# Seven input transfers per head pair in place of twelve, in a fused attention and two-MLP kernel

## Chip, cores and metric

The kernel runs on one core of a Trainium2 chip. The metric is the device time of one execution in microseconds (us). The kernel before was run three times: 1204.57, 1206.59 and 1207.52 us, a median of 1206.59.

## What is computed

Three stages follow each other: attention with a threshold, then two layers of a gated MLP form. All inputs and outputs are fp32.

```
scores = q k^T / sqrt(64)                      (batch 4, heads 8, seq 576, dim 64)
scores below max - tau are dropped; attn = softmax(scores); a = attn v
x   = a as (2304 tokens, 512)
x1  = (s * relu(x @ w_in)^2 + b) @ w_out         (512 -> 2048 -> 512)
h   = x1 @ w2_in;  out = (h * tanh(softplus(h))) @ w2_out
```

## The kernel before, in words

Attention works on **pairs** of heads: 4 batches of 4 pairs, 16 pairs in all. A pair's queries are handled in 9 ticks of 128 columns (`scores`, lines 236 to 279): ticks 0 to 3 are head 0, ticks 5 to 8 are head 1, and tick 4 holds the last 64 queries of both. A tick's exponentials are transposed seven ticks later (`weights_t`, line 283) and multiplied with v one tick after that (`product`, line 303). After the last product of a pair, `split_x` (line 314) writes its result as a high and a low part.

For precision, fp32 products are made of fp32r parts: an operand is split into `hi` (rounded) and `lo` (the rest). For each pair `prep_qk` (line 196) does this for k and for q. TensorE transposes the raw tile in five pieces of 128 columns (line 204), which ends in the PSUM tile `tpk` or `tpq`. `load_raw` for the following pair is issued (line 205). ScalarE copies 576 columns to `hi` (line 208) and VectorE subtracts to get `lo` (line 209). Then `move` brings halves of 64 partitions to the tiles `Q`, `KH` and `KL` of one of two sets (`self.sets`, lines 139 to 148). For the first pair (`pr` 0) the moves are copies on ScalarE, VectorE and GpSimd (lines 228 to 232); for all others they are DMAs on the SP queue (line 226): six for k, and six for q, since head 1 of q is cut in two pieces per half.

`load_raw` (line 160) brings a pair's raw tiles: k in 5 transfers (lines 176 and 184 to 187), q in 3 (lines 176, 178, 179), v in 4 (lines 171 to 173), all on the SP queue. In `attention` (line 324) the k and q of pair 0 are loaded first (line 332), then three scalars, then v. In the loop the next pair's k is prepared after tick 2, its q after tick 4, and its v is loaded after tick 8 (lines 349 to 354). The v tiles are two buffers, so the v of pair p goes into the tile that pair p-2 used.

The first stage of the program runs attention for pairs 0 to 3 alone, beside a generator that reads weights (`split_w`, line 46): one DMA into `wraw` (line 57), one pass on ScalarE (line 62), three on VectorE (lines 64 to 66), a copy on ScalarE (line 69) and a subtraction on GpSimd (line 70). These pieces are used in the first MLP (`moe1`, line 151, its products in line 403), which from pair 4 on is woven with attention in a fixed proportion (lines 612 to 626). For batches 1 to 3 the split weights come back from DRAM (`w<-w`, line 395). When attention is done, the weights of the second MLP are split, and `moe2` (line 469) runs at the end.

Every engine, and the SP queue, takes its instructions in order. The order in each of them is not the program's alone: the build places instructions by a timeline of its own, with the program's order as priority (line 687).

```
687    with _tile.TileContext(nc, schedule_with_timeline_sim=True) as tc:
```

Of the kernel before, what the change touches and what calls it, by code (L numbers as in the profile page):

```python
# [8 lines left out]
F32 = mybir.dt.float32  # L9
# [10 lines left out]
class Fused:  # L20
# [12 lines left out]
    def consts(self, pool):  # L33
        nc = self.nc
        i2 = pool.tile([P, 192], F32, name="ident")
        self.ident, self.swap = i2[:, 0:128], i2[:, 64:192]
        make_identity(nc, self.ident)
        nc.gpsimd.tensor_copy(i2[:, 128:192], i2[:, 0:64])
        self.tau_c = pool.tile([P, 1], F32, name="tau_c")
        self.s_c = pool.tile([P, 1], F32, name="s_c")  # L40
        self.b_c = pool.tile([P, 1], F32, name="b_c")
        self.colsum = pool.tile([P, 4], F32, name="colsum")
        self.cb = pool.tile([P, 4], F32, name="cb")
# [88 lines left out]
    def attn_alloc(self):  # L132
        nc = self.nc
        self.sets = []

# [13 lines left out]
        self.qk = {}  # L149
        for n in "qk":  # L150
            t = self.qk[n] = self.at.tile([P, 5, 2, 64], F32, name=f"raw{n}", bufs=1)
            nc.gpsimd.memset(t[64:128, 4], 0.0)
# [7 lines left out]
    def load_raw(self, pr, nm):  # L160
# [4 lines left out]
        src = {"q": self.q, "k": self.k, "v": self.v}[nm]  # L165
        h2 = src[b, 2 * p:2 * p + 2]
        rem = h2[:, 512:576, :].rearrange("h r d -> r h d")
        if nm == "v":
            t = self.vs[pr % 2]
            for h in range(2):  # L170
                nc.sync.dma_start(t[:, h, 0:4, :], h2[h, 64 * h:64 * h + 512, :].rearrange("(p c) d -> p c d", c=4))
            nc.sync.dma_start(t[0:64, 0, 4, :], h2[0, 512:576, :])
            nc.sync.dma_start(t[64:128, 1, 4, :], h2[1, 0:64, :])
        else:
            t = self.qk[nm]
            nc.sync.dma_start(t[:, 0:4, 0, :], h2[0, 0:512, :].rearrange("(p c) d -> p c d", c=4))
            if nm == "q":
                nc.sync.dma_start(t[:, 0:4, 1, :], h2[1, 0:512, :].rearrange("(p c) d -> p c d", c=4))
                nc.sync.dma_start(t[0:64, 4, :, :], rem)
            else:  # L180


                full = h2[1, 64:576, :].rearrange("(p c) d -> p c d", c=4)
                nc.sync.dma_start(t[64:128, 0:4, 1, :], full[0:64])
                nc.sync.dma_start(t[0:64, 1:5, 1, :], full[64:128])
                nc.sync.dma_start(t[0:64, 0, 1, :], h2[1, 0:64, :])
                nc.sync.dma_start(t[0:64, 4, 0, :], h2[0, 512:576, :])
# [7 lines left out]

    def prep_qk(self, pr, n):


        nc = self.nc
        raw = self.raws.pop((pr, n))  # L200
        Q, KH, KL, _ = self.sets[pr % 2]
        tp = self.s_tile(f"tp{n}{pr}")
        for c in range(5):
            nc.tensor.transpose(tp[:, c * 128:c * 128 + 128], raw[:, c].rearrange("p h d -> p (h d)"), self.ident)
        self.load_raw(pr + 1, n)
        hi = self.at.tile([P, 576], F32R, tag="hi", name=f"hi{n}{pr}", bufs=1)
        lo = self.at.tile([P, 576], F32R, tag="lo", name=f"lo{n}{pr}", bufs=1)
        nc.scalar.copy(hi, tp[:, :576])
        nc.vector.tensor_tensor(lo, tp[:, :576], hi.bitcast(F32), op=ALU.subtract)
        for h, (own, oth) in enumerate((HALVES, HALVES[::-1])):  # L210
            for half, t in ((own, hi), (oth, hi if n == "k" else lo)):
                if n == "k":
                    parts = [(KH[h], 0, 576, 0)]
                else:
                    parts = [(Q, 0, 576, 0)] if h == 0 else [(Q, 0, 512, 704), (Q, 512, 576, 128)]
                for dst, a, z, o in parts:
                    self.move(pr, dst[half, a + o:z + o], t[own, a:z], t is hi)
            if n == "k":
                self.move(pr, KL[h][own, :], lo[own, :], None)

    def move(self, pr, dst, src, early):


        nc = self.nc
        if pr:
            nc.sync.dma_start(dst.bitcast(F32), src.bitcast(F32))
        elif early is None:
            nc.gpsimd.tensor_copy(dst, src.bitcast(F32))
        elif early and dst.shape[-1] > 64:
            nc.scalar.copy(dst, src.bitcast(F32))  # L230
        else:
            nc.vector.tensor_copy(dst, src.bitcast(F32))
# [91 lines left out]
    def attention(self):  # L324
# [11 lines left out]
        self.load_raw(0, "v")  # L336
        for n in "kq":
            self.prep_qk(0, n)
        fin = todo = None
        tes = {}  # L340
        for k in range(N + LAG + 2):
            pr, ti = divmod(k, 9)
            if k < N:
# [5 lines left out]
                if pr + 1 < self.B * self.NP and ti in (2, 4, 8):  # L349
                    if ti == 8:  # L350
                        self.load_raw(pr + 1, "v")
                    else:
                        self.prep_qk(pr + 1, "kq"[ti // 2 - 1])
                        yield 500
# [8 lines left out]
            if todo:  # L363
# [8 lines left out]
                if tc == 8:  # L372
                    self.split_x(tp)
            todo = (prj, ci, tnew) if 0 <= j < N else None
# [317 lines left out]
```

## Time and profile before

| | |
|---|---|
| median of three runs | 1206.59 us |
| the profiled execution, its own time | 1204.01 us |
| its span, first to last instruction | 1201.8 us |
| TensorE busy | 1145.2 us, 95% |
| VectorE / ScalarE / GpSimd busy | 626.1 / 529.7 / 427.3 us |

In the rows, PE is TensorE, PEld its weight loads, DVE is VectorE, ACT is ScalarE, POOL is GpSimd, and SPq the issuing queue of SyncE. L204 is line 204. A busy PE is not a PE at its peak, since matmuls are pipelined and their ends are modelled; the distance between starts tells what one costs in a stream. A releaser is inferred from semaphore events.

### The profile page before, as it was taken

How to read it: one execution, taken by the hardware profiler on the slowest of the kernel's cores; microseconds unless marked ns; L12 is line 12 of the kernel's file. 1: busy time of each engine (PE TensorE's matmuls, PEld its weight loads, DVE VectorE, ACT ScalarE, POOL GpSimd, SP SyncE). 2: the span in 40 equal slices, each digit the busy share in tenths (PEclk: the TensorE clock that was granted, in tenths of full speed). 3: DMA queues.
4: the chain of work that ended last, by engine and by line, in shares of the span. 5: the costliest groups of instructions: out<-in, count | busy, mean ns of one | idle time of the engine just before them, and what ended most of it. 6: DMA issues, size and time to landing. Idle time of an engine off the chain costs nothing.

```text
span 1201.8 us, 19799 instructions
## 1 busy us (share of the span) xinstructions
PE 1145.2 (95%) x7104; PEld 979.2 (81%) x7104; DVE 626.1 (52%) x1505; ACT 529.7 (44%) x1073; POOL 427.3 (36%) x600
## 2 busy tenths in 40 slices
PE   4888999898899999999999999999999999999998
PEld 4666888877678998988988999878888888888886
DVE  5888777878885464655552689964111111111111
ACT  4666666575655544445533465553221221222211
POOL 4566777776644334326422344432000000000000
PEclk8989999999999999999999999999999999999999
DMA  5657466576595455374423898763030020030000
GB/s 128 166 136 183 110 217 184 159 207 173 170 289 156 158 154 159 125 233 140 136 86 106 256 324 283 276 230 105 1 105 1 1 70 1 1 105 1 19 1 35
DMA packets 123667, 161.84 MB, mean 135 GB/s; under 512 B 57393, under 2 KB 78897, under 8 KB 123569
## 3 DMA queue, kind: packets, MB, share of 16 engines
q1 hardware_dynamic: 123568, 160.58, 43.5%
q8 instruction: 56, 0.92, 0.3%
q14 instruction: 43, 0.34, 0.1%
HBM read 107.48 MB, written 30.93 MB: 115 GB/s over the span
## 4 chain that ended last, share of the span: by engine, by line
PE 69%; DMA 10%; DVE 8%; POOL 5%; issue 3%; ACT 2%; SPq 2%; DVEq 0%; ACTq 0%; POOLq 0%
PE o L522 17%; PE h L403 11%; PE y L403 10%; PE hm L493 8%; PE hp L493 8%; PE pv L311 6%; DMA wraw<-in_moe_w_in_dram 4%; PE S L252 4%; DMA wraw<-in_moe_w_out_dram 4%; PE T L289 3%; POOL e L277 3%; DVE wa L64 1%; DMA w<-w 1%; DVE wa L65 1%; DVE wa L66 1%
## 5 line engine op out<-in xcount | busy, mean ns | idle before, releaser
L507 DVE TENSOR_TENSOR g2l<-t,g2h 128x512 fp32r<-128x512 f32 (+1 forms) x80 | 51.9, 648 | 315.4 <-ACT t L506 311.6
L403 PE MATMUL y<-gh,w 128*128 128x288 f32 x768 | 164.6, 300 | 3.1 <-DVE y L450 2.9
L403 PE MATMUL h<-xh,w 128*128 128x288 f32 x768 | 165.5, 301 | 1.9 <-DMA w<-w 1.7
L522 PE MATMUL o<-w2o,g2h 128*128 128x512 f32 x576 | 150.0, 395 | 1.9 <-ACT g2h L505 1.9
L267 DVE SCALAR_TENSOR_TENSOR e<-ns,st,e 128x576 f32<-128x576 f32 x128 | 119.2, 935 | 47.3 <-ACT e L263 33.4
L277 POOL TENSOR_SCALAR e<-e,st 128x576 f32<-128x576 f32 x128 | 127.5, 1005 | 32.3 <-DVE st L272 26.1
L256 DVE TENSOR_SCALAR_CACHE_REDUCE ns<-S 128x576 f32<-128x576 f32 x144 | 107.7, 751 | 54.2 <-PE S L252 53.3
L403 PEld LDWEIGHTS y<-gh,w 128*128 128x128 f32 x768 | 125.8, 188 | 11.1 <-issue 4.4
L403 PEld LDWEIGHTS h<-xh,w 128*128 128x128 f32 x768 | 125.9, 188 | 9.5 <-issue 5.7
L263 ACT ACTIVATE e<-ns,st 128x576 f32<-128x576 f32 x128 | 98.8, 776 | 70.9 <-DVE ns L256 59.6
L522 PEld LDWEIGHTS o<-w2o,g2h 128*128 128x128 f32 x576 | 107.0, 188 | 26.7 <-ACT g2h L505 2.3
L300 ACT COPY te<-T 128x576 f32<-128x576 f32 x144 | 91.1, 632 | 66.6 <-PE T L294 60.5
L258 POOL TENSOR_SCALAR st<-st,tau_c 128x1 f32<-128x1 f32 x144 | 61.1, 426 | 164.9 <-DVE ns L256 140.7
L403 PE MATMUL y<-gl,w 128*128 128x288 f32 x384 | 113.8, 297 | 0.5 <-DVE gl L427 0.5
L252 PE MATMUL S<-KH,Q 128*128 128x288 f32 x320 | 100.3, 329 | 14.6 <-DVE ns L256 5.0
L403 PE MATMUL h<-xl,w 128*128 128x288 f32 x384 | 113.8, 297 | 0.0
L289 PE MATMUL T<-ident,e 128*128 128x128 f32 x576 | 98.3, 279 | 13.8 <-ACT te L300 8.6
L493 PE MATMUL hm<-y,w2i 128*128 128x512 f32 (+1 forms) x480 | 108.4, 372 | 0.0
L493 PE MATMUL hp<-y,w2i 128*128 128x512 f32 (+1 forms) x480 | 107.2, 372 | 0.0
L427 POOL TENSOR_TENSOR gl<-rr,gh 128x288 fp32r<-128x288 f32 x96 | 80.6, 845 | 73.8 <-DVE rr L426 63.2
L311 PE MATMUL pv<-te,rawv 128*64 128x288 f32 x640 | 105.6, 420 | 0.0
L493 PEld LDWEIGHTS hm<-y,w2i 128*128 128x128 f32 x480 | 84.5, 188 | 18.0
(94 smaller groups left out, 2122.7 us busy)
## 6 DMA issues: line engine op xcount, KB each, us to landing
w<-w SPq DMA_DIRECT2D x96, 512.0 KB, 4.2
wraw<-in_moe_w_in_dram SPq DMA_DIRECT2D x64, 256.0 KB, 3.9
w<-wp SPq DMA_DIRECT2D x32, 512.0 KB, 4.0
wraw<-in_moe_w_out_dram SPq DMA_DIRECT2D x64, 256.0 KB, 4.4
KH<-hik SPq DMA_DIRECT2D x60, 144.0 KB, 2.5
y<-yT SPq DMA_DIRECT2D x32, 256.0 KB, 4.0
KL<-lok SPq DMA_DIRECT2D x30, 144.0 KB, 2.7
rawq<-in_q_dram SPq DMA_DIRECT2D x32, 128.0 KB, 3.0
```

What stands on the lines that cost most here:

```text
L252: nc.tensor.matmul(so, Q[:, c0:c0 + 128], kt[:, ks], start=(i == 0), stop=(i == len(terms) - 1))
L256: nc.vector.tensor_scalar(ns.rearrange("p (h n) -> p h n", h=2), sv, -0.125, 3.0e38, op0=ALU.mult, op1=ALU.min, accum_out=nm[:, c1])
L263: nc.scalar.activation(e, ns, AF.Exp, bias=nm[:, c1], scale=-1.0)
L267: nc.vector.scalar_tensor_tensor(e, ns, nthr[:, c1], e, op0=ALU.is_le, op1=ALU.mult, accum_out=sm[:, c1])
L277: nc.gpsimd.tensor_scalar(t, t, rinv[:, j:j + 1], u[:, j:j + 1], op0=ALU.mult, op1=ALU.add)
L289: nc.tensor.transpose(T[:, i * 128:i * 128 + 128], self.es[pr, i, "pair"][:, o:o + 128], self.ident)
L300: nc.scalar.copy(te, T[:, :576])
L311: self.nc.tensor.matmul(self.pv[HALVES[h], hf * HB:hf * HB + 288], v[:, h, c, :], tes[h][:, hf * 288:hf * 288 + 288], start=first, stop=last)
L403: nc.tensor.matmul(acc[:, :n], w[:, wl, c], rhs[c][xl][:, ts], start=(i == 0), stop=(i == 11))
L427: (nc.vector if b == 3 else nc.gpsimd).tensor_tensor(gl[:, ts], r2, gh[:, ts].bitcast(F32), op=ALU.subtract)
L493: nc.tensor.matmul(hp[:, :n], w[:, wl, kc, fs], yy[kc], start=(i == 0), stop=(i == 11))
L522: nc.tensor.matmul(outs[t], g[:, t * 128:t * 128 + 128], w[:, wl, fc % 4, :], start=(fc == 0 and i == 0), stop=(fc == 15 and i == 2))
```

## The change

The raw k and q tiles come in two transfers each (512 rows of both heads, then the last 64 rows of both), the v tile in three. q of pair 0 is issued from ScalarE's queue, all else from SP. Head 1's rows are now stored in the same order as head 0's. So that each head's 576 columns are contiguous after the transposes, the 64 remaining columns are produced twice, at both ends, by two ordinary matmuls with 64 columns of the identity in place of the fifth transpose; `hi` and `lo` grow from 576 to 640 columns. The q of head 1 then needs two moves in place of four, ten moves a pair in all. The first pair is prepared by a function of its own: both transposes first, head 0 moved by engines, head 1 by DMAs on SP. v of pairs 0 and 1 is loaded at the start, and v of pair p+2 right behind `split_x` of pair p. Five small tiles become slices of one.

```diff
@@ attn_alloc
+        self.qk = {}
+        for n in "kq":
+            t = self.qk[n] = self.at.tile([P, 5, 2, 64], F32, name=f"raw{n}", bufs=1)
+            nc.gpsimd.memset(t[64:128, 4], 0.0)
...
@@ load_raw
+        dma = nc.scalar if nm == "q" and not pr else nc.sync
         h2 = src[b, 2 * p:2 * p + 2]
+        most = h2[:, 0:512, :].rearrange("h (p c) d -> p c h d", c=4)
         if nm == "v":
             t = self.vs[pr % 2]
+            nc.sync.dma_start(t[:, :, 0:4, :], most.rearrange("p c h d -> p h c d"))
             for h in range(2):
-                nc.sync.dma_start(t[:, h, 0:4, :], h2[h, 64 * h:64 * h + 512, :].rearrange("(p c) d -> p c d", c=4))
-            nc.sync.dma_start(t[0:64, 0, 4, :], h2[0, 512:576, :])
-            nc.sync.dma_start(t[64:128, 1, 4, :], h2[1, 0:64, :])
+                nc.sync.dma_start(t[HALVES[h], h, 4, :], h2[h, 512:576, :])
         else:
             t = self.qk[nm]
...
+            dma.dma_start(t[:, 0:4], most)
+            dma.dma_start(t[0:64, 4, :, :], h2[:, 512:576, :].rearrange("h r d -> r h d"))
@@
+    def raw_t(self, pr, n):
+        nc = self.nc
+        raw = self.raws.pop((pr, n))
+        tp = self.s_tile(f"tp{n}{pr}")
+        for c, o in ((4, 192), (0, 256), (1, 384), (2, 512), (3, 640), (4, 768)):
+            rows = raw[:, c].rearrange("p h d -> p (h d)")
+            if c < 4:
+                nc.tensor.transpose(tp[:, o:o + 128], rows, self.ident)
+            else:
+                nc.tensor.matmul(tp[:, o:o + 64], rows, self.ident[:, 0:64], start=True, stop=True)
+        self.load_raw(pr + 1, n)
+        return tp
+
+    def parts(self, pr, n, tp, tags):
+        nc = self.nc
+        hi, lo = (self.at.tile([P, 1152 if t == "e" else 640], F32R, tag=t, name=f"{w}{n}{pr}",
+                               bufs=8 if t == "e" else 1)[:, :640] for w, t in zip(("hi", "lo"), tags))
+        nc.scalar.copy(hi, tp[:, 192:832])
+        nc.vector.tensor_tensor(lo, tp[:, 192:832], hi.bitcast(F32), op=ALU.subtract)
+        return hi, lo
+
+    def moves(self, pr, n, h, hi, lo):
+        Q, KH, KL, _ = self.sets[pr % 2]
+        own, oth = HALVES[h], HALVES[1 - h]
+        cols = slice(64 - 64 * h, 640 - 64 * h)
+        out = []
+        for half, t in ((own, hi), (oth, hi if n == "k" else lo)):
+            dst = KH[h] if n == "k" else Q[:, 640 * h:640 * h + 576]
+            out.append((dst[half, :], t[own, cols]))
+        return out + ([(KL[h][own, :], lo[own, cols])] if n == "k" else [])
+
     def prep_qk(self, pr, n):
...
+        hi, lo = self.parts(pr, n, self.raw_t(pr, n), ("hi", "lo"))
+        for h in range(2):
+            for dst, src in self.moves(pr, n, h, hi, lo):
+                self.nc.sync.dma_start(dst.bitcast(F32), src.bitcast(F32))
+
+    def prep_first(self):
+        nc = self.nc
+        tps = [self.raw_t(0, n) for n in "kq"]
+        (kh, kl), (qh, ql) = (self.parts(0, n, tp, tags) for n, tp, tags in
+                              zip("kq", tps, (("hi", "lo"), ("e", "e"))))
+        k0, k1, k2 = self.moves(0, "k", 0, kh, kl)
+        q0, q1 = self.moves(0, "q", 0, qh, ql)
+        nc.scalar.copy(k0[0], k0[1].bitcast(F32))
+        nc.gpsimd.tensor_copy(k1[0], k1[1].bitcast(F32))
+        nc.gpsimd.tensor_copy(k2[0], k2[1].bitcast(F32))
+        nc.scalar.copy(q0[0], q0[1].bitcast(F32))
+        nc.vector.tensor_copy(q1[0], q1[1].bitcast(F32))
+        for n, hi, lo in (("k", kh, kl), ("q", qh, ql)):
+            for dst, src in self.moves(0, n, 1, hi, lo):
+                nc.sync.dma_start(dst.bitcast(F32), src.bitcast(F32))
@@ attention
-        self.load_raw(0, "v")
-        for n in "kq":
-            self.prep_qk(0, n)
+        for pr in range(2):
+            self.load_raw(pr, "v")
+        self.prep_first()
...
-                if pr + 1 < self.B * self.NP and ti in (2, 4, 8):
-                    if ti == 8:
-                        self.load_raw(pr + 1, "v")
-                    else:
-                        self.prep_qk(pr + 1, "kq"[ti // 2 - 1])
-                        yield 500
+                if pr + 1 < self.B * self.NP and ti in (2, 4):
+                    self.prep_qk(pr + 1, "kq"[ti // 2 - 1])
+                    yield 500
...
                 if tc == 8:
                     self.split_x(tp)
+                    self.load_raw(tp + 2, "v")
```

## Rows read from the trace of the kernel before

**Rows 1.** The page, part 1: busy time, share of the span, instructions.
```profile
PE 1145.2 (95%) x7104; PEld 979.2 (81%) x7104; DVE 626.1 (52%) x1505; ACT 529.7 (44%) x1073; POOL 427.3 (36%) x600
```

**Rows 2.** The table by stretch (stretch: length, busy and count per engine, PE clock, DMA share, GB/s).
```profile
30.00:60.00 30.00, 25.48 (x161) 18.63 (x160) 25.83 (x74) 19.26 (x34) 16.82 (x26) 0.94 0.61 166
...
90.00:120.00 30.00, 25.43 (x177) 18.31 (x175) 24.87 (x71) 19.30 (x33) 20.66 (x28) 1.00 0.71 184
130.00:400.00 270.00, 252.83 (x1810) 217.75 (x1809) 202.08 (x504) 163.88 (x338) 182.86 (x257) 1.00 0.62 187
400.00:600.00 200.00, 200.00 (x1484) 180.96 (x1482) 113.34 (x277) 98.31 (x182) 83.92 (x117) 1.00 0.52 156
```

**Rows 3.** The chain that ended last, 0 to 65 us: start, length, what.
```profile
0.72 0.70 SPq L176
...
4.73 3.23 DMA rawq<-in_q_dram
...
8.09 1.27 PE tpq L204 x5
...
10.07 0.65 ACT hiq L208
...
10.97 0.77 DVE loq L209
...
12.36 2.27 PE S L252 x8
...
20.09 2.30 PE S L252 x8
...
28.03 0.43 SPq L226
...
32.98 3.02 DMA wraw<-in_moe_w_in_dram
```

**Rows 4.** Waits of ACT, 0 to 130 us (total us, times, longest).
```profile
ACT wraw L62 <- DMA wraw<-in_moe_w_in_dram: 6.0, 5, 2.1
```

**Rows 5.** Waits of ACT, 130 to 400 us.
```profile
ACT wraw L62 <- DMA wraw<-in_moe_w_out_dram: 14.0, 17, 1.7
...
ACT wraw L62 <- DMA wraw<-in_moe_w_in_dram: 7.7, 13, 1.6
```

**Rows 6.** The SP queue in order of time, 0 to 140 us: start, length, line, transfer.
```profile
15.83 0.94 SPq L171 DMA_DIRECT2D rawv<-in_v_dram  x2
...
31.71 0.59 SPq L173 DMA_DIRECT2D rawv<-in_v_dram  x1
```

**Rows 7.** DMA issues by kind: count, KB of each, median us from issue to landing.
```profile
wraw<-in_moe_w_in_dram SPq DMA_DIRECT2D x64, 256.0 KB, 3.9
...
KH<-hik SPq DMA_DIRECT2D x60, 144.0 KB, 2.5
```

**Rows 8.** TensorE in order of time near 634 us; rows overlap, the starts count.
```profile
634.27 0.27 PE L289 MATMUL T<-ident,e 128*128 128x128 f32 x1
634.38 0.33 PE L297 MATMUL T<-ident,E 128*128 128x64 f32 x2
634.55 0.39 PE L298 MATMUL T<-ident,E 128*128 128x64 f32 x2
634.74 0.38 PE L403 MATMUL h<-xh,w 128*128 128x288 f32 x1
```

**Rows 9.** The table by stretch for line 204 alone.
```profile
0.00:130.00 130.00, 11.79 (x60) 9.34 (x60) 0.92 0.58 152
130.00:400.00 270.00, 8.67 (x60) 6.97 (x60) 1.00 0.62 187
400.00:600.00 200.00, 5.78 (x40) 4.59 (x40) 1.00 0.52 156
```

**Rows 10.** Line 209 on DVE, by shape: count, busy us, mean ns.
```profile
L209 DVE TENSOR_TENSOR loq<-tpq,hiq 128x576 fp32r<-128x576 f32 x16 | 12.1, 755 | 7.6 <-ACT hiq L208 7.5
```

**Rows 11.** Waits of the SP queue, whole run (total us, times, longest).
```profile
SPq L171 <- PE pv L311: 9.5, 7, 3.7
```

More of the change, by code (lines that the diff above doesn't have):

```diff
@@ L38, in consts @@
         nc.gpsimd.tensor_copy(i2[:, 128:192], i2[:, 0:64])
[L39 to L43, printed above, removed]
+        small = pool.tile([P, 11], F32, name="small")
+        self.tau_c, self.s_c, self.b_c = (small[:, i:i + 1] for i in range(3))
+        self.colsum, self.cb = small[:, 3:7], small[:, 7:11]
     def split_w(self, src, hi, lo, pool, tags, kw):
@@ L148, in attn_alloc @@
             self.sets.append((Q, KH, KL, e4[:, g * 640:g * 640 + 704]))
[L149 to L152, printed above, removed]
         self.vs = []
@@ L194, in s_tile @@
         return pool.tile([P, 1024], F32, tag="S", name=name)
-    def prep_qk(self, pr, n):
+    def raw_t(self, pr, n):
         nc = self.nc
         raw = self.raws.pop((pr, n))
-        Q, KH, KL, _ = self.sets[pr % 2]
[L202 to L219, printed above, removed]
@@ L221, in move @@
-    def move(self, pr, dst, src, early):
-        nc = self.nc
[L225 to L232, printed above, removed]
+        tp = self.s_tile(f"tp{n}{pr}")
[5 more added lines that the diff above has]
+                nc.tensor.matmul(tp[:, o:o + 64], rows, self.ident[:, 0:64], start=True, stop=True)
@@ new lines, in prep_qk @@
+    def prep_qk(self, pr, n):
+        hi, lo = self.parts(pr, n, self.raw_t(pr, n), ("hi", "lo"))
[3 more added lines that the diff above has]
+    def prep_first(self):
+        nc = self.nc
+        tps = [self.raw_t(0, n) for n in "kq"]
[11 more added lines that the diff above has]
+                nc.sync.dma_start(dst.bitcast(F32), src.bitcast(F32))
@@ L348, in attention @@
                 yield 550
-                if pr + 1 < self.B * self.NP and ti in (2, 4, 8):
-                    if ti == 8:
-                        self.load_raw(pr + 1, "v")
-                    else:
-                        self.prep_qk(pr + 1, "kq"[ti // 2 - 1])
-                        yield 500
+                if pr + 1 < self.B * self.NP and ti in (2, 4):
+                    self.prep_qk(pr + 1, "kq"[ti // 2 - 1])
+                    yield 500
             elif fin:
```

10 lines of the change are left out of this document (removed).

## The prediction

> **What bounds the kernel now.** The page first: TensorE is busy 95% of the span [rows 1]. The table by stretch shows that this average hides three regimes [rows 2]. Between 400 and 600 us TensorE is busy all 200 of 200 us: there the time is the sum of its matmuls. Between 130 and 400 us it is busy 252.8 of 270 us, so 17.2 us are waits. In the first 130 us, where attention runs alone for pairs 0 to 3, the two windows shown have it busy 25.4 and 25.5 us of 30 with far fewer matmuls (177 and 161, where the stretch from 400 us has 1484 in 200 us, some 223 per 30). VectorE is busy 24.9 and 25.8 us of 30 there, about 84%. That stretch is a net of short waits around VectorE, and here an earlier transfer can move something.
>
> The chain that ended last shows which [rows 3]. Until 12.36 us everything waits for the first pair: SP issues k and then q one after the other from 0.72 us, q's second piece is issued at 4.73 us and takes 3.23 us, the transposes of q start at 8.09 us, `hi` at 10.07, `lo` at 10.97, the first scores at 12.36. From 28.03 us eight SP issues stand in a row on the chain: five moves of q, two small pieces of v, one weight transfer, which is itself on the chain from 32.98 us for 3.02 us. ScalarE waits for such weight pieces 6.0 us in the first 130 us [rows 4] and 14.0 + 7.7 us between 130 and 400 us [rows 5]. An issue holds the SP queue some 0.6 us (a small v piece 0.59, two large ones 0.94) [rows 6].
>
> **The change, part by part.**
>
> *Start.* A k load of 256 KB is issued at 0.72 us. The nearest row, a 256 KB weight load, lands in 3.9 us [rows 7], so k is there at about 4.6. q goes out on ScalarE's queue beside it, not after five issues, so q is there before TensorE has finished k. Five transposes took 1.27 us in the start [rows 3]; which is about twice five times the 0.11 us of later (below), so I count the two ordinary products at twice 0.25 us too and take 1.77 us each for k and q: done at about 6.5 and 8.2. `hi` of 640 columns is 0.72 us (0.65 x 640/576) and `lo` 0.85 (0.77 x 640/576), both from the chain's lengths; the last copy to the first scores takes 0.62 us as before (10.97 + 0.77 to 12.36). That gives 10.4 in place of 12.36, **-1.9 us**. Bounds: both loads together are 512 KB; from 144 KB in 2.5 us to 256 KB in 3.9 us [rows 7] a KB adds 0.0125 us, so q could land 3.2 us later, at 7.8: then only 0.5 us is won. If k lands in 2.5 + 0.7 us, 2.6 us is won. I take 1.9, nearest to the 256 KB row. Head 1's moves of the first pair, now DMAs, are covered: some 20 SP issues of 0.6 us from 0.72 us on end at 12.7 us, and with 2.5 us of landing [rows 7] at 15.2, while the tick that needs head 1 stood at 20.09 us [rows 3]. Without that cover tick 4 would wait for them, late by as much as they land after it. The v of pair 1, loaded early, is used only by pair 1's products and costs nothing but its place in that queue, counted among the 20.
>
> The row shows q late because its issue stood behind five others. The Trainium skill, "DMA: Bandwidth & Descriptors", section "Issuing engines are not separate DMA queues", says that transfers from different issuers share the same 16 engines and that a second issuer saves only issue time; by that, k and q would share the engines fully, the start would give the lower bound of 0.5 us, and the sum would be +1.2 us.
>
> *SP time.* Per pair 12 + 12 issues become 7 + 10: seven fewer, 7 x 0.6 = 4.2 us of queue. It counts only where the chain runs through the queue. In the run at 28.03 us two moves and two v pieces go, 2.4 us; other pairs have shorter runs, and what is late next is VectorE, which is 84% busy. The lower bound is 0. For the upper bound I take the ScalarE waits for weights, 6.0 + 21.7 = 27.7 us, of which a third at most can come through, since VectorE and GpSimd follow in the same chain: 9 us. I take **-3.0 us**, a little over what the one run shows. An issue of a merged load has no row; it lies between 0.6 us (one load) and 1.25 us (the two that it replaces). I take 0.65, since rows of very different size all lie at 0.4 to 0.6; at 1.25 the saving per pair falls from 4.2 to 2.4 us and this term to -1.7.
>
> *TensorE.* One transpose becomes two ordinary fp32 products with 64 columns. The kernel already has this pair: lines 297 and 298 show two instructions for each such product, and the four of them run from 634.38 to 634.74 us, 0.36 us, while the transpose ahead of them took 634.27 to 634.38, 0.11 us [rows 8]. So each preparation costs TensorE 0.25 us more. By five transposes each, 12 preparations lie in the first 130 us, 12 in 130 to 400, 8 in 400 to 600 [rows 9]. The last eight are paid in full, 2.0 us. Of 12 x 0.25 = 3.0 us I count two thirds, 2.0, since part falls into TensorE's 17.2 us of waits. In the first stretch I take nothing; the cover is TensorE's 4.5 us of idle time in each 30 [rows 2], and without it 10 x 0.25 = 2.5 us come on top (the first two are in the start). Sum **+4.0 us**, ends +2.0 and +7.5.
>
> The Trainium skill, "TensorE: Matmul & The Clock Gate", section "Terms", gives the transpose mode as four times faster for fp32. By this, the 128 ordinary columns would cost four times the transpose of 128, 0.44 us in place of 0.11, and the term would be +5.3; the rows give 0.36 us for the same columns, and the measurement decides.
>
> *VectorE and ScalarE.* `lo` is 755 ns for 576 columns [rows 10], so 64 more cost 0.084 us; ten preparations in the stretch where VectorE is 84% busy make 0.8 us, times 0.84: **+0.7 us** (ends 0 and 0.8). ScalarE, 19.3 us of 30 in both windows, has room for its 0.07.
>
> *v later or earlier.* The load now stands right behind the last product, whose end it must wait for. What queues behind it on SP are k's moves and the weights. Before, such waits came to 9.5 us in 7, the longest 3.7 [rows 11]; I take no change, ends 0 and +4.5 (see the rivals). The merged constants and the order of memsets I cost at nothing: GpSimd's memsets lie beside the first loads, and were they not covered, at most 1 us of start would go.
>
> Sum: -1.9 - 3.0 + 4.0 + 0.7 = -0.2 us. The profiled execution took 1204.01 us, 2.6 below the median of 1206.59; so 1203.8 beside it, **1206.4** against the median, which I round to 1206.5. A measurement of this kernel can tell about 0.3%, 3.6 us, from no change.
>
> **The rivals.**
> - *The queue was worth more.* Relief in the first 400 us reaches 8 us, and the start gives 2.6; of TensorE's 130 to 400 us only 1.0 us of the addition shows: -2.6 - 8 + 3.0 + 0.5 = -7.1, **1199.5**. For it: eight SP issues in one run of the chain, ScalarE's 27.7 us of waits for weights. Against: VectorE at 84%, and SP's relief ends where VectorE is late.
> - *TensorE is the bound and the ordinary products decide (slower).* If the waits of the first 400 us belong to VectorE and GpSimd, SP time is worth nothing: start -0.5, products 30 x 0.25 = +7.5, `lo` +0.7: +7.7, **1214.3**. It decides from the point at which relief is under half of what the products add. For it: TensorE without any idle time for 200 us. Against: the first 130 us, where TensorE has idle time.
> - *The new v load holds the queue.* If it stops SP 3.7 us in each pair and so takes away the relief and adds 1.5 us: -1.9 + 4.0 + 0.7 + 1.5 = +4.3, **1210.9**. Against: seven such waits in sixteen pairs, most short.
> - *The change does not shorten the queue,* since merged issues last as long as those that they replace: relief 1.7, sum +1.1, 1207.7; that is within no change.
>
> The build orders all engines by a timeline of its own: the two larger v pieces of pair 1 were issued at 15.83 us, its last small one at 31.71 [rows 6], though the code has them side by side. So a changed queue shuffles the rest too. I have no price for it; it widens the range by some 3 us on both sides of the forecast.
>
> **How the numbers follow.** No change, as summed, 0.41 (its own range 1203 to 1210); the queue worth more 0.36; TensorE deciding 0.15; the v load 0.08. So faster 0.36, within 0.3% 0.41, slower 0.23. The range reaches from 1198 (just beyond the first rival) to 1213 (just short of the second), and leaves out about 2 in 10.
>
> **What would show it.** Right: the first scores at 10 to 11 us; line of the products with 0.25 us more per preparation and TensorE's stretch of full use longer by 2 us or more; ScalarE's waits for weights fewer by 3 us or more. Wrong: first scores not before 11.9; TensorE's idle time between 130 and 400 us falling well under 10 us, or the first stretch shorter by more than 6 us (then the queue was worth more); long SP waits of the v load.

## The result and the profile after

The changed kernel takes 1214.70 us (median of 4 runs, 1213.88 to 1215.87), the kernel before 1206.96 us beside it on the same chip: a ratio of 1.0073, 95% interval 1.0059 to 1.0086. It is 7.7 us slower. The profiled executions took 1215.15 and 1204.01 us, with spans of 1213.4 and 1201.8 us.

Part 1 of the page of the kernel after; it answers to [rows 1].

```profile
PE 1155.6 (95%) x7200; PEld 993.4 (82%) x7200; DVE 641.2 (53%) x1502; ACT 528.3 (44%) x1069; POOL 421.5 (35%) x600
```

TensorE has 96 instructions and 10.4 us more. The rest of the span, its idle time, went from 1201.8 - 1145.2 = 56.6 to 57.8 us. To see where, the span is cut at the same events in each kernel: the first product of the first MLP, 400 us, attention's last `x` piece (after it attention is over), and the first product `o` of the second MLP. In each row the first two numbers are the stretch and its length, then TensorE's busy time; their difference is its idle time. The table by stretch, kernel before:

```profile
0.00:130.10 130.10, 102.19 (x621) 75.98 (x621) 98.85 (x278) 76.05 (x129) 76.51 (x133) 0.92 0.58 152
130.10:400.00 269.90, 252.73 (x1810) 217.75 (x1809) 201.98 (x504) 163.78 (x337) 182.86 (x257) 1.00 0.62 187
400.00:656.00 256.00, 256.00 (x1888) 228.29 (x1886) 136.53 (x330) 119.79 (x221) 100.89 (x142) 1.00 0.47 143
656.00:802.60 146.60, 140.09 (x1002) 135.19 (x1002) 117.03 (x273) 78.65 (x200) 53.26 (x56) 1.00 0.82 275
```

and kernel after:

```profile
0.00:130.90 130.90, 107.06 (x657) 82.04 (x657) 99.86 (x276) 76.02 (x126) 76.49 (x133) 0.93 0.62 156
130.90:400.00 269.10, 251.39 (x1822) 223.57 (x1822) 204.49 (x466) 154.72 (x332) 176.31 (x247) 0.99 0.62 188
400.00:688.90 288.90, 288.44 (x2150) 257.82 (x2149) 155.26 (x387) 133.92 (x238) 106.87 (x158) 1.00 0.52 154
688.90:813.20 124.30, 113.12 (x786) 106.87 (x786) 109.42 (x254) 72.19 (x188) 51.15 (x52) 1.00 0.78 258
```

The event that moved most is attention's end, from 656.0 to 688.9 us. More products of the first MLP now stand ahead of it; it is 2322 of 3072, where it was 2106. The stage behind it is shorter, and holds 11.2 us of idle time in place of 6.5. The stretch from the first product to 400 us idles 17.7 us, as before (17.2).

Two parts of the change can be read directly. The start, from the chain of waits, TensorE in order of time, and the SP queue:

```profile
0.72 0.77 SPq L175 DMA_DIRECT2D rawk<-in_k_dram  x1
```

```profile
1.55 4.59 DMA rawk<-in_k_dram
```

```profile
6.27 0.66 PE L195 MATMUL tpk<-ident,rawk 128*128 128x64 f32 x2 [6.27 <-DMA rawk<-in_k_dram]
...
11.92 0.82 PE L262 MATMUL S<-KH,Q 128*128 128x288 f32 x2 [2.22 <-DVE Q L239]
```

The merged load's issue holds SP 0.77 us, k lands at 6.1 us, and the first scores start at 11.92 us instead of 12.36 [rows 3]. And one preparation amid other work, at a place where a product of the MLP stands ahead of it and attention's transposes behind it, in order of time: before, then after.

```profile
458.54 0.71 PE L204 MATMUL tpk<-ident,rawk 128*128 128x128 f32 x5
459.09 0.60 PE L289 MATMUL T<-ident,e 128*128 128x128 f32 x4
```

```profile
459.39 0.33 PE L195 MATMUL tpk<-ident,rawk 128*128 128x64 f32 x2
459.56 0.61 PE L193 MATMUL tpk<-ident,rawk 128*128 128x128 f32 x4
460.00 0.33 PE L195 MATMUL tpk<-ident,rawk 128*128 128x64 f32 x2
460.17 0.61 PE L299 MATMUL T<-ident,e 128*128 128x128 f32 x4
```

From start to start it was 459.09 - 458.54 = 0.55 us and is 460.17 - 459.39 = 0.78, so 0.23 us more. What stands beside a preparation matters: between products with v it is 0.69 and 0.98 us, 0.29 more. Times 32 that is 7.4 to 9.3 us of the 10.4 by which TensorE's busy time rose. The rest need not be work, since busy time moves with the order too: e8 below adds no TensorE instruction to the kernel before and is busy 1153.1 us.

### The profile page after: what moved, and what is told of

It is laid out like the page before. It is cut to its first block, busy times and chain, and to the rows that moved or that the text cites. A ratio compares the mean times of both kernels' runs of the same rounds, so it can differ in the third digit from the quotient of the medians.

```text
span 1213.4 us, 19823 instructions
## 1 busy us (share of the span) xinstructions
PE 1155.6 (95%) x7200; PEld 993.4 (82%) x7200; DVE 641.2 (53%) x1502; ACT 528.3 (44%) x1069; POOL 421.5 (35%) x600
## 4 chain that ended last, share of the span: by engine, by line
PE 69%; DVE 9%; DMA 8%; POOL 5%; issue 4%; ACT 3%; SPq 0%; DVEq 0%; ACTq 0%; POOLq 0%
PE o L530 17%; PE y L411 10%; PE h L411 9%; PE hm L501 8%; PE hp L501 8%; PE pv L321 6%; PE S L262 5%; DMA wraw<-in_moe_w_in_dram 4%; PE T L299 4%; DMA wraw<-in_moe_w_out_dram 3%; DVE wa L63 2%; POOL e L287 2%; DVE wa L62 1%; DVE e L277 1%; DVE wa L64 1%
## 5 line engine op out<-in xcount | busy, mean ns | idle before, releaser
L268 POOL TENSOR_SCALAR st<-st,small 128x1 f32<-128x1 f32 x144 | 56.7, 395 | 178.0 <-DVE ns L266 149.4
## 6 DMA issues: line engine op xcount, KB each, us to landing
wraw<-in_moe_w_in_dram SPq DMA_DIRECT2D x64, 256.0 KB, 3.8
wraw<-in_moe_w_out_dram SPq DMA_DIRECT2D x64, 256.0 KB, 3.3
y<-yT SPq DMA_DIRECT2D x32, 256.0 KB, 4.3
```

## The experiments

All are timed against the kernel before on the same chip; the chips differ from run to run, so the ratios are what compares, and they carry their 95% intervals. Two theories stood at first. **P**: the ordinary products are extra work for a TensorE that is the bound. **H**: attention ends later, and the stage behind it is then too short to be filled.

### One part at a time

**e1**, the kernel after with the last 64 rows through transposes of 64 rows in place of the products:

```diff
-                nc.tensor.matmul(tp[:, o:o + 64], rows, self.ident[:, 0:64], start=True, stop=True)
+                nc.tensor.transpose(tp[:, o:o + 64], raw[0:64, c].rearrange("p h d -> p (h d)"), self.ident[0:64, 0:64])
```

> The changed kernel, with the two ordinary 64-column products of a preparation replaced by two transposes of the 64 valid partitions. Theory P (the ordinary products decide): TensorE's preparation falls from about 0.80 us to 0.44 to 0.66 us, 32 of them, so 4 to 8 us come back: 1207 to 1210.5. Theory H (attention ends 33 us later beside the first MLP, and the stretch behind it, where VectorE splits the second MLP's weights, is too short): TensorE's order has attention's last product behind 2322 of 3072 products of the first MLP, as in the changed kernel (2106 before), so attention still ends near 685 us and at most 3 us come back: 1212 to 1215.

1210.79 us, ratio 1.0038 (1.0026 to 1.0050). But it did not make a preparation cheaper; TensorE in order of time:

```profile
506.98 0.27 PE L195 MATMUL tpq<-ident,rawq 64*128 64x64 f32 x1
507.19 0.66 PE L193 MATMUL tpq<-ident,rawq 128*128 128x128 f32 x4
507.77 0.27 PE L195 MATMUL tpq<-ident,rawq 64*128 64x64 f32 x1
507.98 0.44 PE L299 MATMUL T<-ident,e 128*128 128x128 f32 x2
```

One of 64 rows takes 0.21 us, the four full ones between them 0.58 instead of 0.44, together 1.00 us, more than the 0.78 with the products. It won about 4 us with more work on TensorE, which already speaks against P.

**e2** and **e3** put one part each into the kernel before: e2 the products, e3 the wider copies and the merged constants.

```diff
-        for c in range(5):
+        for c in range(4):
...
+        for o in (512, 640):
+            nc.tensor.matmul(tp[:, o:o + 64], raw[:, 4].rearrange("p h d -> p (h d)"), self.ident[:, 0:64], start=True, stop=True)
```

> The kernel before, with only the fifth transpose of a preparation replaced by the two ordinary 64-column products. Theory P: 32 x 0.25 = +8 us, 1213 to 1216. Theory H: the order shifts too, attention's last product stands behind 2274 products of the first MLP in place of 2106, which alone would cost some 3 to 5 us; with the products' work on top 1211 to 1219. A result within 2 us of before would sink P.

```diff
...
-        nc.scalar.copy(hi, tp[:, :576])
-        nc.vector.tensor_tensor(lo, tp[:, :576], hi.bitcast(F32), op=ALU.subtract)
+        nc.scalar.copy(hi, tp[:, :640])
+        nc.vector.tensor_tensor(lo, tp[:, :640], hi.bitcast(F32), op=ALU.subtract)
...
```

> The kernel before, with only hi and lo widened to 640 columns (and the five small tiles in one, which makes the room). No ordinary product is added. Theory P: at most +1 us, 1206 to 1208. Theory H: attention's last product stands behind 2298 products of the first MLP in place of 2106, so attention ends some 25 us later and the time rises by 3 to 6 us, 1210 to 1213.

e2: 1212.04 us, 1.0048 (1.0031 to 1.0065). e3: 1211.79 us, 1.0048 (1.0032 to 1.0065). Each alone costs about 6 us, and the change, which holds both and more, costs 7.7. e3 adds no work to TensorE (1146.7 us busy), yet attention's end moved to 681.0 us, and the stage behind it idles 13.0 us:

```profile
681.00:809.20 128.20, 115.17 (x810) 109.78 (x810) 109.57 (x255) 73.53 (x189) 47.47 (x52) 0.99 0.81 267
```

**e4** asks whether VectorE is what that stage waits for: the kernel after, with 32 squares moved to GpSimd.

```diff
-                    (nc.vector if b > 0 else nc.gpsimd).tensor_tensor(r2, r, r, op=ALU.mult)
+                    (nc.vector if b in (1, 2) else nc.gpsimd).tensor_tensor(r2, r, r, op=ALU.mult)
```

> The changed kernel, with the squares of the last batch's first MLP (line 434, 32 of 0.45 us) on GpSimd in place of VectorE; TensorE's order is as in the changed kernel. Theory H: VectorE bounds the stretch from 740 to 790 us, so taking up to 14 us of work from it gives back 3 us or more, 1209 to 1212. Theory P: VectorE decides nothing there, within 1.5 us of the changed kernel, 1213 to 1216.

1218.06 us, 1.0097 (1.0073 to 1.0121), so no gain (after has 1.0073, up to 1.0086). VectorE had 33 instructions fewer in the stage and hardly less busy time (109.0 us for 109.4), since its others grew longer; so the run took nothing off VectorE and does not settle what it asked. Line 62 over the whole run, after and e4 (busy us, mean ns):

```profile
L62 DVE TENSOR_SCALAR wa<-wraw 128x256 int32<-128x256 int32 x128 | 53.5, 420 | 33.5 <-ACT wraw L60 15.0 <-POOL wp L68 12.5 <-POOL gl L435 2.4
```

```profile
L62 DVE TENSOR_SCALAR wa<-wraw 128x256 int32<-128x256 int32 x128 | 57.6, 453 | 34.1 <-ACT wraw L60 20.9 <-POOL wp L68 12.3 <-POOL w2o L68 0.6
```

### Edits that hardly do anything but move the order

Four edits of the kernel before. e5 sets attention's priority offset to 0, e6 lets attention lead by 10000 instead of 5000, e7 merges q's two large loads, e8 puts pair 0's q on ScalarE's queue (with a lead of 15000, so that the order stays close to that of before).

```diff
-                with tc.high_priority(offset=200):
+                with tc.high_priority(offset=0):
```

> The kernel before with one number changed: attention's priority offset 200 becomes 0. Every instruction stays; only the build's order differs, and attention's last product stands behind 2274 products of the first MLP in place of 2106. Theory H (a late end of attention leaves the stretch behind it too short): attention ends near 680 us, and the time rises by 4 to 7 us, 1209 to 1213. Theory P (the ordinary products and the wider copies, as work): no work is added, so the time stays within 2 us of before.

```diff
-            if a_on and (not m_on or (a_done - 5000.0) / a_left <= m_done / m_left):
+            if a_on and (not m_on or (a_done - 10000.0) / a_left <= m_done / m_left):
```

> The kernel before with attention's lead in the program's weave 10 us in place of 5 us; same instructions, attention's last product behind 2227 products. Theory H, with the slope of the widened kernel (6.4 us for 192 products): +4.0 us, attention's end near 670 us, 1208 to 1211. Theory P: within 2 us of before.

```diff
-            nc.sync.dma_start(t[:, 0:4, 0, :], h2[0, 0:512, :].rearrange("(p c) d -> p c d", c=4))
...
-                nc.sync.dma_start(t[:, 0:4, 1, :], h2[1, 0:512, :].rearrange("(p c) d -> p c d", c=4))
+                nc.sync.dma_start(t[:, 0:4], h2[:, 0:512, :].rearrange("h (p c) d -> p c h d", c=4))
...
```

> The kernel before, with only the two large q loads of a pair merged into one: 15 SP issues fewer, no added work on any engine. The build's order has attention's last product behind 2298 products. Theory H: +4 to +6.5 us, 1209 to 1212, although the queue is relieved. The prediction's view that SP time is worth something: -0.5 to -1 us, 1204 to 1206.

```diff
-            if a_on and (not m_on or (a_done - 5000.0) / a_left <= m_done / m_left):
+            if a_on and (not m_on or (a_done - 15000.0) / a_left <= m_done / m_left):
...
-            nc.sync.dma_start(t[:, 0:4, 0, :], h2[0, 0:512, :].rearrange("(p c) d -> p c d", c=4))
+            dma = nc.scalar if nm == "q" and not pr else nc.sync
+            dma.dma_start(t[:, 0:4, 0, :], h2[0, 0:512, :].rearrange("(p c) d -> p c d", c=4))
...
```

> The kernel before, with the first pair's three q loads on ScalarE's queue and attention's lead 15 us, which brings attention's last product to 2130, near the 2106 of before. Theory H: +0.8 us for the 24 products, less what the start gives (first scores 0.4 to 1.5 us earlier): 1204 to 1206.5. If the start is worth its full gain in time, this is the fastest version so far.

| run | products ahead of attention's end | median us (before: 1206.45) | ratio to before |
|---|---|---|---|
| e5 | 2274 | 1210.01 | 1.0014 (0.9996 to 1.0031) |
| e6 | 2227 | 1207.91 | 0.9999 (0.9982 to 1.0017) |
| e7 | 2298 | 1207.07 | 1.0011 (0.9994 to 1.0029) |
| e8 | 2130 | 1212.08 | 1.0046 (1.0033 to 1.0060) |

So the number of products ahead is not what costs: e7 has nearly after's and loses at most 0.3%, e8 has nearly before's and loses 5.6 us, of which its first scores, 1.1 us later than before's, can explain a small part. (e5 lies 3.6 us up by its median, and its interval leaves it open.) H in its first form falls.

### Parts of the change taken back

**e9** uses full transposes for the last rows, **e10** cuts the 7 transfers into 12, **e11** leaves pair 0's q on SP, **e12** puts the v loads back.

```diff
-            if c < 4:
-                nc.tensor.transpose(tp[:, o:o + 128], rows, self.ident)
-            else:
-                nc.tensor.matmul(tp[:, o:o + 64], rows, self.ident[:, 0:64], start=True, stop=True)
+            nc.tensor.transpose(tp[:, o:o + 128], rows, self.ident)
```

> The kernel after, but chunk 4 goes through two transposes of the full tile (128 rows, 128 columns, the second half of them zeros or overwritten) instead of two ordinary products of 64 columns. What is computed stays the same, and so does the order of every instruction of TensorE. Theory P (the two products are extra work for a TensorE that has no idle time): a preparation goes from 0.88 us to six transposes of 0.11, 0.66 us, so 32 x 0.22 = 7.0 us go, and the time is about 1207.7, 1.0 us above the kernel before. Theory H (the order in which TensorE gets its work, with 2322 of 3072 products of the first MLP ahead of attention's last product and a short stage behind it that nothing fills): the order is as in the kernel after, so the end of attention moves from 689 to about 682 us, the stage behind keeps its 124 to 128 us, and all of the 7 us is won only if nothing in that stage is late: 1208 to 1214. P falls if the time stays at 1213 or more while TensorE's busy time falls by 6 us or more.

```diff
-            nc.sync.dma_start(t[:, :, 0:4, :], most.rearrange("p c h d -> p h c d"))
+                nc.sync.dma_start(t[:, h, 0:4, :], h2[h, 0:512, :].rearrange("(p c) d -> p c d", c=4))
...
-            dma.dma_start(t[:, 0:4], most)
-            dma.dma_start(t[0:64, 4, :, :], h2[:, 512:576, :].rearrange("h r d -> r h d"))
+            for h in range(2):
+                dma.dma_start(t[:, 0:4, h, :], h2[h, 0:512, :].rearrange("(p c) d -> p c d", c=4))
+                dma.dma_start(t[0:64, 4, h, :], h2[h, 512:576, :])
```

> The kernel after, with q, k and v of a pair in 12 transfers again (each of the seven cut by head, so that a partition's piece and the place in the tiles stay as they are in the kernel after). TensorE's order is the same as after's. The theory that the seven transfers win time on SP's queue: 5 issues of about 0.6 us per pair come back, which is 3 us per pair of a queue that the wide copies wait on; the time goes up by 1 to 3 us, to 1215.7 to 1217.7. The rival, that the queue was never late by enough to be the last to end: within 1 us of the kernel after. In the first 12 us, k in two loads of 128 KB instead of one of 256 KB may also start the transposes at another time, by 0.5 us to either side.

```diff
-        dma = nc.scalar if nm == "q" and not pr else nc.sync
+        dma = nc.sync
```

> The kernel after, with pair 0's q loads on SP's queue behind k's, instead of on ACT's. TensorE's order is the same. The theory that the second queue only moves the k transposes later, as both loads share the transfer engines: k lands about 0.9 us earlier, q about as late as its issue, and the first product of S comes at 11.9 plus or minus 0.7 us: the time within 0.7 us of the kernel after. The rival, that the second queue saves q's issue time: the first S 0.7 to 1.5 us later, and the time by as much.

```diff
-        for pr in range(2):
-            self.load_raw(pr, "v")
+        self.load_raw(0, "v")
...
+                    if ti == 8:
+                        self.load_raw(pr + 1, "v")
...
-                    self.load_raw(tp + 2, "v")
```

> The kernel after, with the v loads back at the place they have in the kernel before (tile 8 of the pair before; only pair 0's at the start). TensorE's order is the same. The theory that the new place makes SP wait: SP's waits on pv for a v load fall from 24 us in 10 waits back to the 11.9 us of the kernel before or less, with the wide loads behind them on time, and the time falls by 0.5 to 4.5 us, to 1210 to 1214. The rival, that these waits end before anything is due: within 1 us of the kernel after.

e9: 1206.14 us, 0.9992 (0.9984 to 1.0001). e10: 1207.24 us, 1.0003 (0.9992 to 1.0015). e11: 1213.21 us, 1.0049 (1.0035 to 1.0063). e12: 1214.25 us, 1.0061 (1.0048 to 1.0073).

Two unlike edits, each alone, bring back the whole 7.7 us, which no sum of costs can explain. e10 gives SP's queue more to issue and leaves TensorE's busy time as it is in after (1156.8 us); its gain is in the stretch from the first product to 400 us, 9.9 us idle instead of 17.7:

```profile
133.70:400.00 266.30, 256.38 (x1868) 227.98 (x1868) 201.60 (x479) 159.57 (x337) 179.88 (x254) 0.99 0.64 193
```

The expectations say that TensorE's order is the same. That was read off the one count, 2322, and it does not hold. Of the 1696 matmuls of attention's scores, transposes and products, 889 stand behind another number of MLP products in e9 than in after (between 21 fewer and 36 more), 1108 in e10, 1200 in e12, and none in e11. So e9, e10 and e12 mix an edit with a new order, and so does e1 (1018).

In e11, whose TensorE order is unchanged, k lands in 3.04 us instead of 4.59, and the first scores start at 10.38 us, 1.5 us earlier than with the second queue:

```profile
1.55 3.04 DMA rawk<-in_k_dram
```

```profile
10.38 0.82 PE L262 MATMUL S<-KH,Q 128*128 128x288 f32 x2 [2.22 <-DVE Q L239]
```

In e12 the SP queue's waits for a pair's last product stayed at 39 us (41 us in after), because the build sets the place of the loads in the queue; the old place in the program is not the old place in the queue, and the run tells nothing of that wait.

### The order held

For e13 to e16 the order was taken out of one program and held in another. Between neighbours in that order an edge is added on the engine, which fixes who is issued first:

```diff
+def keep_order(nc, tc, orders):
...
+    for e, order in orders.items():
+        for a, b in zip(order, order[1:]):
+            tc.add_manual_dep(by[e][b], by[e][a].name,
+                              mybir.DependencyInfo(mybir.DependencyClass.NoSync, mybir.DependencyReason.DATA),
+                              reason="order")
...
         attention_two_moes(tc, *args)
+        keep_order(nc, tc, orders_from(ORDER_TEXT, COUNTS))
```

In e13 all five engines are held, in e14 to e16 four of them: SP's queue and the first pair's own copies, which differ between the programs, are left to the build. In the traces, TensorE's scores, transposes, products with v and MLP products stand in e15 as they do in before, and in e13 as they do in after. Theory **O**: what costs the time is the order that the build makes of the changed program.

> The kernel of e9 (chunk 4 through full transposes instead of two ordinary products) with every instruction of all five engines held in the place it has in the kernel after. Theory P (the products are work on a TensorE that is never idle from 400 us on): 32 preparations x 0.22 us = 7 us less than the kernel after, about 1207.7. Theory O (the order that the build makes is what costs the time, and e9 won because it got another one): 1213 to 1215, as the kernel after. Between 1209 and 1212: both, in shares that the number gives.

> The kernel before, its own work and transfers, with TensorE, VectorE, ScalarE and GpSimd held in the order of the kernel after (the five transposes of a preparation stand where the six instructions stand there; the first pair's own copies and the issue order of SP's queue are left to the build). Theory O: 1212 to 1215, most of the 7.8 us appears without any of the change's edits. Theory P: 1205.5 to 1208, as the kernel before, since five transposes of 0.11 us do not depend on their place.

> The kernel after with TensorE, VectorE, ScalarE and GpSimd held in the order of the kernel before (the six instructions of a preparation stand where the five transposes stand there; the first pair's own copies and SP's queue are left to the build). Theory O: 1205 to 1209. Theory P: the products still cost 32 x 0.33 = 10.6 us against the kernel before, less the 0.4 to 1 us won at the start: 1213 to 1217.

> The kernel after with its 7 transfers, and with TensorE, VectorE, ScalarE and GpSimd held in the order of e10, which has 12. Theory O: about 1207, as e10. The theory that seven transfers with longer pieces arrive later, or hold the queue longer, than twelve short ones: 1213 to 1215, as the kernel after.

| run | work | order | median us | ratio to before |
|---|---|---|---|---|
| after | after | after | 1214.70 | 1.0073 (1.0059 to 1.0086) |
| e13 | e9 | after | 1213.44 | 1.0069 (1.0049 to 1.0089) |
| e15 | after | before | 1206.26 | 1.0008 (0.9996 to 1.0021) |
| e16 | after | e10 | 1207.02 | 1.0005 (0.9990 to 1.0021) |
| e14 | before | after | 1238.14 | 1.0266 (1.0241 to 1.0290) |

Beside after, before took 1206.96 us; beside e13 to e16 it took 1205.74.

e13 is the test of P. A preparation is cheaper in it, at the place shown above 460.03 - 459.37 = 0.65 us in place of 0.78, and TensorE's busy time fell by 4 us to 1151.5:

```profile
459.37 0.82 PE L192 MATMUL tpk<-ident,rawk 128*128 128x128 f32 x6
460.03 0.60 PE L296 MATMUL T<-ident,e 128*128 128x128 f32 x4
```

So P asks for 32 x 0.13 = 4 us less than after (the expectation has 7), a ratio of about 1.0038. The time stayed: 1213.44 us, 1.0069, with a lower end of 1.0049. P falls as the cause of the whole loss, though with the intervals of both runs the products could by e13 alone still cost some 3 us. What e9 won came with its order. e15 is the whole change, products, wide copies, 7 transfers and v place, in the order of before, and it costs 0.5 us by the medians, with an interval from -0.5 to +2.5, where P asks for 32 x 0.25 = 8 us (the expectation has 10.6). e16 has the 7 transfers in the order of e10, and runs like e10. By e15 the edits cost little, and the order costs 7 to 8 us (7.7 less 0.5 by the medians, 0.0065 or 7.8 us by the ratios). e13, held and slow, shows that holding an order does not by itself make a program fast; that a program held in its own order keeps its time was not tried beyond that. Which engine's order it is was not separated either, and SP's queue was free in e15 and e16.

Where the order costs it: e15 by stretch, to be set beside the table of after,

```profile
0.00:129.20 129.20, 106.07 (x658) 81.59 (x658) 99.92 (x277) 75.09 (x126) 76.41 (x133) 0.92 0.61 158
129.20:400.00 270.80, 257.75 (x1833) 222.80 (x1833) 199.65 (x500) 161.39 (x334) 181.40 (x257) 0.98 0.63 186
400.00:659.60 259.60, 259.60 (x1924) 232.09 (x1923) 137.66 (x332) 121.91 (x224) 101.14 (x143) 1.00 0.47 141
659.60:805.20 145.60, 139.18 (x1003) 134.92 (x1003) 117.20 (x273) 78.64 (x200) 54.14 (x56) 1.00 0.81 277
```

and e16's second stretch and its last:

```profile
134.20:400.00 265.80, 258.00 (x1882) 229.08 (x1882) 201.88 (x483) 161.28 (x339) 181.99 (x255) 0.99 0.65 195
...
679.60:804.40 124.80, 113.09 (x786) 106.79 (x786) 108.20 (x254) 71.99 (x188) 53.01 (x52) 1.00 0.77 258
```

e15 is 8.2 us shorter than after in span (1205.2 and 1213.4) with 2.5 us more TensorE time, so it idles 10.7 us less: 4.7 between the first product and 400 us (13.0 and 17.7), 4.8 behind attention's end (6.4 and 11.2), 1.2 in the rest. e16 won in the first of these places alone (7.8 us idle, and 11.7 behind attention's end). The same work can thus idle between 7.8 and 17.7 us in that stretch, by its order.

e14 overshoots both theories. The first product of the MLP comes at 149.0 us, and the SP queue waits 18.9 us for v's buffers in the first 131 us (7.2 in before). Its v loads stand at before's place while the engines follow an order made for earlier ones; that this is the cause is not shown:

```profile
SPq L171 <- PE pv L311: 18.9, 4, 9.6
```

It shows that an order made for one program can be bad for another, though before's order suits the changed program well (e15). As a test of O against P it decides nothing.

### Could the two be had together?

e17 and e18 take the cheapest edits: full transposes, and q on SP (both diffs stand above). e17 holds four engines in the order of before. e18 holds TensorE alone: up to pair 7 the order of e10, behind it MLP products thinned out until 2106 stand ahead of attention's end.

> The kernel after with full transposes for chunk 4 (as e9) and pair 0's q on SP's queue (as e11), with TensorE, VectorE, ScalarE and GpSimd held in the order of the kernel before. By e15 (1206.3), less what e11 and e13 showed against the kernel after (1.5 and 1.3 us, each at the edge of what can be told): 1203.5 to 1206. If the order were not what decides, but the sum of edits: the same as e9 less 1.5, about 1204.6, which this run can't tell apart; it is the control for e18.

> The work of e17, with only TensorE held: up to pair 7 in the order of e10, from there with the products of the first MLP thinned out evenly, so that 2106 of them (as in the kernel before) instead of 2322 stand ahead of attention's last product; the other engines are left to the build. Theory O with its two places: idle time of TensorE from the first product to 400 us 8 to 10 us (e10, e16) instead of e15's 13, and 6.5 us behind attention's end instead of 11 to 12: 3 to 5 us less than e17, 1199 to 1202. The rival, that idle time saved in one place comes back in the other, because VectorE and ScalarE have the same work to do for the same products: as e17, 1203.5 to 1206, with the sum of the two idle times at 18 us or more.

e17: 1205.53 us, 0.9998 (0.9984 to 1.0012). e18: 1208.95 us, 1.0020 (1.0008 to 1.0033). e18 misses: its idle times are 13.2 us in the second stretch and 7.9 in the last, 21.1 together where e17 has 13.8 + 6.3 = 20.1, and the first product came at 138.7 us.

```profile
138.70:400.00 261.30, 248.08 (x1783) 218.01 (x1783) 201.56 (x474) 154.72 (x327) 180.10 (x249) 0.99 0.63 190
...
662.20:810.60 148.40, 140.55 (x1003) 135.25 (x1003) 118.01 (x273) 79.30 (x200) 52.75 (x56) 1.00 0.80 271
```

The sum of the two idle times is what the rival of that expectation says, the time is 3 us above both, and with the other engines left free the run can't tell which of them is to blame. No version beat the kernel before beyond the interval. What makes an order good stays open: neither the number of products ahead (e5 to e8, e16) nor the distance from before's order accounts for the times (of the runs with another order, e8's TensorE stays nearest to before's and loses 5.6 us; e9's is as far from it as after's and loses nothing).

## Why the prediction was wrong, point by point

The step that failed is the last of the rivals' part: "The build orders all engines by a timeline of its own ... I have no price for it; it widens the range by some 3 us on both sides". Its size was 7 to 8 us: the change costs 7.7 us in its own order and 0.5 us in before's (e15). With it the time lies 1.7 us beyond the upper end, 1213. The sum of the edits, -0.2 us, agrees with e15 (+0.5, from -0.5 to +2.5), which is in part luck: the start gave 1.5 us less than its term, and the SP time nothing that can be told. (The one profiled execution each of e15 and before are 3.4 us apart in span; the medians of all executions, 0.5.) Term by term:

- *Start, -1.9.* Measured -0.4 at the first scores, outside the bounds of -0.5 to -2.6 by a little. What was wrong is when k lands, 4.6 us in the prediction and 6.1 measured: k and q were on their way together, and k took 4.59 us where it takes 3.04 in e11. In e11 k does land at 4.6 us, and the first scores start at 10.38, the 10.4 of the prediction, so the rest of that sum held; the transposes and products took 6.27 to 7.89, 1.6 us for k, where it has 1.77. The rule of the Trainium skill ("DMA: Bandwidth & Descriptors", section "Issuing engines are not separate DMA queues") that the prediction set aside agrees with this trace: both issuers share the engines. Its 0.5 us is near the 0.4 measured. One row was misread, without effect on the sum: the 3.23 us from 4.73 us on [rows 3] are the transfer of q's first piece, which SP issued from 4.09 us on.
- *SP time, -3.0.* The relief is there (a merged k load held SP a median of 0.65 us, as the prediction took it, so the last of its rivals falls), and it is worth nothing that these runs can tell. ScalarE's waits for weights in the first 400 us, before and then e15:

```profile
ACT wraw L62 <- DMA wraw<-in_moe_w_out_dram: 15.1, 18, 1.7
ACT wraw L62 <- DMA wraw<-in_moe_w_in_dram: 13.6, 18, 2.1
```

```profile
ACT wraw L60 <- DMA wraw<-in_moe_w_out_dram: 10.0, 11, 2.1
ACT wraw L60 <- DMA wraw<-in_moe_w_in_dram: 7.2, 9, 1.8
```

  That is 28.7 and 17.2 us in the same order of four engines. In the order of e10, 7 transfers (e16) have 18.7 and 12 (e10) 30.7 us, and the times are 1207.02 and 1207.24. Some 12 us of waits went and the time did not move, within some 2 us; so the rival in which the queue is worth 8 us falls, at least in that order. Whether a part came through in e15 can't be told. In after's own order the same seven transfers wait 38.0 us.
- *TensorE, +4.0.* The price held: 0.23 to 0.29 us more for each preparation, where the prediction has 0.25. The two products take 0.17 us each, 0.34 in all, where [rows 8] gave 0.36. The rule that the prediction weighed and set aside, transposes four times faster for fp32 (the Trainium skill, "TensorE: Matmul & The Clock Gate", section "Terms"), would give 4 x 0.11 = 0.44, and the trace of after does not agree: 0.34 is three times 0.11. Up to 400 us most of the added work falls into idle time: by then e15 has 363.8 us of TensorE's busy time behind it and before 354.9, 8.9 us more, with 8.9 us less idle time, and it is behind by 12 records of other work, about 1.6 us at 0.13 us each. Behind 400 us e15's stage is 3.6 us longer (259.6 and 256.0), which is these 1.6 us and eight preparations of about 0.25. In these two profiles the term of +4.0 is thus near its size. That the full transposes won nothing clear in after's order (e13) need not speak against it: in that order TensorE idles 57.8 us (after), in before's 47.1 (e15).
- *Wider copies, +0.7, and v's place, 0.* Neither was measured by itself in a held order; e15 bounds only the sum of all parts. SP's waits for a pair's last product rose from 11.9 us (9.5 of them in [rows 11]) to 41.2 in after. They are 32.0 us in e15 too, which runs at before's time, so a rise of 20 us has no price there that can be told, and the rival in which the v load holds the queue has nothing for it. After, then e15:

```profile
SPq L170 <- PE pv L321: 27.2, 6, 7.4
SPq L172 <- PE pv L321: 14.0, 7, 4.3
```

```profile
SPq L170 <- PE pv L321: 26.9, 8, 8.7
SPq L172 <- PE pv L321: 5.1, 3, 2.2
```

- *The slower rival* put 1214.3 on the ordinary products, and the time came out there, but by another cause: with the products gone and the order kept (e13) it is still 1213.44. The sign that the prediction gives for its own sum, a stretch of full use longer by 2 us or more, was seen (288.9 us for 256.0) and means something else: 216 MLP products, which stood behind attention's end before, now stand ahead of it.

## What to carry to other kernels

Where a build orders the engines by estimated times, the cost of an edit is the cost of its instructions plus that of a new order, and here the first was about 0.5 us (from -0.5 to +2.5) and the second 7 to 8. Set the two apart by holding one order for both programs before an effect is put down to an edit. Undoing parts one by one misled here: two unlike parts each seemed to carry the whole loss.

## What the runs showed of the hardware that was not expected

- A transpose of 64 rows and 64 columns in a stream of full ones took 0.21 us (e1), a full one of 128 by 128 about 0.11 (0.55 us for five in before), and an ordinary fp32 product of 64 columns 0.17 (after).
- A second issuing queue for the first loads made the first scores 1.5 us later than one queue with q behind k (e8 is in line with that: its first scores start at 13.5 us, in the kernel before at 12.4).
- VectorE's line 62 ran slower beside work on GpSimd. In after it took 286 ns on average in the 62 of 128 times in which GpSimd was busy for less than half of it, and 546 ns in the other 66. With more work on GpSimd (e4) there are 75 of the slow kind, and the average went from 420 to 453 ns.
